# Chunked attention followed by a two-layer MLP: moving the attention output's transposes from TensorE to the DMA engines, and reordering the work around them

## The chip, the cores and the metric

The kernel runs on one core of one Trainium2 chip. The metric is device time in microseconds (us) for one execution. Before the change the median of 7 runs is 247.19 us (246.69 to 248.24). Profile times count from the start of the profiled span.

## The reference

Inputs `q`, `k`, `v` have 4 batches, 8 heads, 768 positions and 64 channels; each head has 8 memory keys and values besides. Each chunk of 32 queries attends to the memory slots and to the keys from 16 before the chunk to 8 after it. The attention output, seen as 3072 tokens of 512 channels, goes through an MLP with hidden width 2048:

```python
scores = scale * (q_c @ k_full.T)             # per batch, head, chunk of 32
a = softmax(scores); attn_out[chunk] = a @ v_full
x = attn_out.transpose(0, 2, 1, 3).reshape(3072, 512)
h = x @ w_in                                  # 512 -> 2048
g = h + sin(alpha * h) ** 2 / alpha
out = g @ w_out                               # 2048 -> 512, float32
```

## The kernel before

The kernel is one program whose order is written by hand; each engine executes its own instructions in the order in which the code records them. Matmul inputs are bf16.

**Stages.** For each of the four batches there are three kinds of work. A *burst* (`burst`) does the attention: 8 blocks of 96 queries. `qk_exp` makes the scores (8 matmuls, tile `sc`) and three exponentials on ScalarE (tile `pt`, line 275). `pv` multiplies by the values (8 matmuls, tile `ot`, line 288); VectorE then takes a reciprocal (L292) and scales into `x_blk` (L293), 96 queries by 512 channels. `xt` transposes `x_blk` on TensorE with four matmuls against an identity (L306) into PSUM, and VectorE copies them into `xT` (L309), which has channels on partitions. *Layer 1* (`l1`, 16 times per batch, once per 128 hidden columns `ft`): 8 matmuls (L341, tile `hT`), a sine on ScalarE (L353), a square into `s2` (letter A: ScalarE, L356; D: VectorE, L358; P: GpSimd), and one fused VectorE instruction (L367, or L363 in halves) that writes `gT`. *Layer 2* (`l2`): 6 groups of 16 matmuls (L393, tile `o`), each group then copied out of PSUM to `o_sb` (L400 VectorE or L402 ScalarE) and stored from SyncE's queue (L403).

**Interleaving.** Layer 2 of batch i is a generator in `stream`; `stream.take(n)` records n of its matmuls. They are spread over the layer 1 of the next batch (2 per `ft`), the burst of the next batch (`shares`, in thirds ahead of, between and behind the parts of a step), and, for batch 0, over the *pieces* of batch 1. A burst step s makes the scores of block s and the values of block s-lag; lag is 2, 3 and 1 for batches 0, 1 and later.

**Pieces.** `q` and `k` come in with positions on partitions. For each of 8 pieces per batch, `pair_up` copies a pair of heads to `pr` (L226), six TensorE transposes (L242 for k, L257 for q) go to a tile `tt_a` or `tt_b`, and VectorE copies k to `kTi` (L243, L249), ScalarE q to `qT` (L258). For batch 1 the pieces stand between layer 1 of batch 0 and burst 1; I call that stretch the *seam*. For batches 2 and 3 they stand between the `l1` calls of the batch before. For batch 0 they open the kernel, with `spin` matmuls on zeros between them.

**PSUM.** Pool `big` has 3 slots of two banks, in rotation, for `sc`, `ot`, `hT` and `tt_b`; pool `smp` has 2 slots of one bank for `o`, `tt_a`, `xtp`, the split `hs` and `spin`. `t_tile` takes `smp` every `state["pools"]`-th time. In the split form of `l1` (batch 0, every fourth `ft`) `hs` takes both `smp` slots.

**Loads.** `load_qk` and `load_v_all` for batch i+2 are issued from GpSimd's queue around burst i+1. They convert float32 to bf16.

Of the kernel before, what the change touches and what calls it, by code (L numbers as in the profile page):

```python
# [9 lines left out]
P = 128  # L10
QW = 96
NEG = -30000.0
KW = 856
BF = mybir.dt.bfloat16
F32 = mybir.dt.float32
ACTF = mybir.ActivationFunctionType
ALU = mybir.AluOpType
# [28 lines left out]
def kernel(  # L46
# [12 lines left out]
    nc = tc.nc  # L59
    B, H, S, D = q.shape  # L60
# [12 lines left out]
    xp = ctx.enter_context(tc.tile_pool(name="xp", bufs=2))  # L73
    gp = ctx.enter_context(tc.tile_pool(name="gp", bufs=2))
    mlp = ctx.enter_context(tc.tile_pool(name="mlp", bufs=3))
    blk = ctx.enter_context(tc.tile_pool(name="blk", bufs=3))
    big = ctx.enter_context(tc.tile_pool(name="big", bufs=3, space=bass.MemoryType.PSUM))
    smp = ctx.enter_context(tc.tile_pool(name="smp", bufs=2, space=bass.MemoryType.PSUM))

# [87 lines left out]
    def spin(n):  # L167

        z = smp.tile([P, 512], F32, name="z", tag="sm")
        for _ in range(n):  # L170
            nc.tensor.matmul(z[:], zeros[:, 0:P], zeros[:])  # L171
# [52 lines left out]
    def pair_up(src, hp, eng=None):  # L224
        pr = blk.tile([P, 6, 2, D], BF, name="pr")
        (eng or nc.gpsimd.tensor_copy)(  # L226
            pr[:].rearrange("p r e d -> p e r d"), src[:, 2 * hp:2 * hp + 2]
        )
        return pr
# [52 lines left out]
    def pv(b, j, pt):  # L282
        x_blk = blk.tile([QW, H, D], BF, name="x_blk")
        rinv = blk.tile([QW, H], F32, name="rinv")
        ot = big.tile([P, 2, 512], F32, name="ot", tag="big")
        otv = ot[:, :, 0:4 * (D + 1)].rearrange("p g (e c) -> p g e c", e=4)
        for h in range(H):
            nc.tensor.matmul(  # L288
                otv[:, h // 4, h % 4, :], pt[:, QW * h:QW * h + P], vws[b % 2][:, h, j, 0:D + 1]
            )  # L290
        rv = rinv[:].rearrange("p (g e) -> p g e", g=2)
        nc.vector.reciprocal(rv, otv[0:QW, :, :, D])  # L292
        nc.vector.tensor_tensor(  # L293
            out=x_blk[:].rearrange("p (g e) d -> p g e d", g=2), in0=otv[0:QW, :, :, 0:D],
            in1=rv.unsqueeze(3).to_broadcast([QW, 2, 4, D]),
            op=ALU.mult,
        )
        return x_blk, ot

    def xt(xT, j, x_blk, ot):  # L300
        if ot is None:
            xtp = smp.tile([P, KT, QW], BF, name="xtp", tag="sm")[:]
        else:
            xtp = ot[:].bitcast(BF)[:, 0, 640:640 + KT * QW].rearrange("p (k c) -> p k c", k=KT)
        for kt in range(KT):
            nc.tensor.transpose(  # L306
                xtp[:, kt, :], x_blk[:, 2 * kt:2 * kt + 2, :].rearrange("p e d -> p (e d)"), ident[0:QW, 0:QW]
            )
        nc.vector.tensor_copy(xT[:, :, QW * j:QW * j + QW], xtp)  # L309

    def burst(b, stream, shares, lag):

        xT = xp.tile([P, KT, S], BF, name="xT")
        ptl, xbl = {}, {}
        for s in range(NJ + lag + 1):
            n = shares[s] if s < len(shares) else 0
            if s < NJ:
                ptl[s] = qk_exp(s)
            if b == 0:
                spin(1)  # L320
            stream.take(n // 3, True)
            if 0 <= s - lag < NJ:
                xbl[s - lag] = pv(b, s - lag, ptl.pop(s - lag))
                if b == 0:
                    xbl[s - lag] = (xbl[s - lag][0], None)
            stream.take((n + 1) // 3, True)
            if 0 <= s - lag - 1 < NJ:
                xt(xT, s - lag - 1, *xbl.pop(s - lag - 1))
            stream.take((n + 2) // 3, True)
        return xT  # L330


    def l1(i, ft, xT, gT, sq, split=False):
        if split:
            hts = [smp.tile([P, 512], F32, name="hs", tag="sm") for _ in range(2)]
        else:
            hT = big.tile([P, 2, 512], F32, name="hT", tag="big")
            hts = [hT[:, 0], hT[:, 1]]
        for kt in range(KT):
            for hf in range(2):  # L340
                nc.tensor.matmul(  # L341
                    hts[hf][:, 0:HALF],
                    w_in_sb[:, kt, P * ft:P * ft + P],
                    xT[:, kt, HALF * hf:HALF * hf + HALF],
                    start=(kt == 0), stop=(kt == KT - 1),
                )
        u = mlp.tile([P, 2, HALF], F32, name="u")
        if split:
            for hf in range(2):
                nc.scalar.activation(  # L350
                    u[:, hf], hts[hf][:, 0:HALF], ACTF.Sin, scale=alpha_sb[:, ft:ft + 1])
        else:
            nc.scalar.activation(u[:], hT[:, :, 0:HALF], ACTF.Sin, scale=alpha_sb[:, ft:ft + 1])  # L353
        s2 = mlp.tile([P, 2, HALF], F32, name="s2")
        if sq == "A":
            nc.scalar.activation(s2[:], u[:], ACTF.Square)  # L356
        else:
            (nc.vector if sq == "D" else nc.gpsimd).tensor_tensor(  # L358
                out=s2[:], in0=u[:], in1=u[:], op=ALU.mult)
        gv = gT[:, ft, :].rearrange("p (e c) -> p e c", e=2)  # L360
        for hf in range(2):
            if split:
                nc.vector.scalar_tensor_tensor(  # L363
                    out=gv[:, hf], in0=s2[:, hf], scalar=inv_alpha[:, ft:ft + 1],
                    in1=hts[hf][:, 0:HALF], op0=ALU.mult, op1=ALU.add)
            elif hf == 0:
                nc.vector.scalar_tensor_tensor(  # L367
                    out=gv, in0=s2[:], scalar=inv_alpha[:, ft:ft + 1],
                    in1=hT[:, :, 0:HALF], op0=ALU.mult, op1=ALU.add)

    def l2(i, gT, last=False):
        for s in range(NSUB):
# [31 lines left out]
            yield True  # L404


    first = (nc.vector.tensor_copy, nc.scalar.copy)
    prs = [pair_up(kq[n], 0, first[n]) for n in range(2)]
    for n in range(2 * HP):
        (t_k if n % 2 == 0 else t_q)(prs[n], n // 2)  # L410
        spin(2)
        if n == 1:
            nc.scalar.copy(memv_st[64:72], memv_f[64:72])
            mt = smp.tile([P, HP, 32], BF, name="mt", tag="sm")
            for hp in range(HP):
                nc.tensor.transpose(
                    mt[:, hp, :],
                    memk_bf[0:32, 2 * hp:2 * hp + 2, :].rearrange("p e d -> p (e d)"),
                    ident[0:32, 0:32])
        if n + 2 < 2 * HP:  # L420
            prs.append(pair_up(kq[n % 2], (n + 2) // 2, first[n % 2]))
        if n == 1:
            nc.vector.tensor_copy(memkT[:], mt[:])
            put_memk(0)
        if n == 3:
            put_memv(0)
    put_memv(1)
    nc.vector.reciprocal(inv_alpha[:], alpha_sb[:])
    for c in range(8):
        load_w_in(c)  # L430
# [5 lines left out]
    stream = Stream()  # L436
    xT = burst(0, stream, (), 2)
    put_memk(1)

    for i in range(B):  # L440
        gT = gp.tile([P, FT, S], BF, name="gT")
        last = i == B - 1
        at_ft = {2 * n: n for n in range(8)}
        pieces = []
        if not last:
            srcs = [(kq_next[n % 2], n // 2) for n in range(2 * HP)]
        state["pools"] = 1

        def pair_to(n):
            while len(pieces) < min(n, 2 * HP):  # L450
                pieces.append(pair_up(*srcs[len(pieces)], nc.vector.tensor_copy if i == 0 else None))

        def piece(n):
            pair_to(n + 3)
            (t_k if n % 2 == 0 else t_q)(pieces[n], n // 2)

        if 0 < i < B - 1:
            pair_to(2)
        for ft in range(FT):
            sq = ("ADADADAA" if i == 0 else "ADADADAA")[ft % 8]  # L460
            if 1 <= ft:
                stream.take(3 if last else 2)
            if 0 < i < B - 1 and ft in at_ft:
                piece(at_ft[ft])
            if i == 0 and ft == 14:
                pair_to(3)
            l1(i, ft, xT, gT, sq, i == 0 and ft % 4 == 3)
        stream.add(l2(i, gT, last))
        if not last:
            if i == 0:  # L470
                state["pools"] = 3
                for n in range(2 * HP):
                    piece(n)
                    stream.take(4)
            if i + 2 < B:
                kq_next = load_qk(i + 2)
            if i == 0:
                xT = burst(i + 1, stream, (3,) * 11, 3)
            else:
                xT = burst(i + 1, stream, (12, 9, 6, 6, 6, 6, 6, 5, 5, 5), 1)  # L480
            if i + 2 < B:
                put_memk(i + 2)
            stream.take(3)
            if i + 2 < B:
                load_v_all(i + 2)
                put_memv(i + 2)
# [31 lines left out]
```

## Time and profile before

| what | value |
|---|---|
| median of 7 runs | 247.19 us (246.69 to 248.24) |
| the profiled execution's own time | 247.48 us |
| its span | 245.8 us |
| mean granted TensorE clock | 0.993 |
| L393 layer-2 matmuls, 368 | 99.9 us busy |
| L341 layer-1 matmuls (`hT`), 480 | 86.2 us busy |
| L306 transposes of `x_blk`, 128 | 10.8 us busy, of which 32 belong to batch 0 |
| L309 copies to `xT`, 32 | 11.1 us busy (346 ns each) |
| chain that ended last | PE 51%, DVE 20%, ACT 15%, issue 6%, POOL 5%, DMA 1% |

PE is TensorE, PEld its weight loads, DVE VectorE, ACT ScalarE, POOL GpSimd, SP SyncE. Busy time of PE counts pipelined matmuls with modelled ends that overlap, so what a matmul costs is better read from the distance between the starts of neighbours in a dense stretch. An arrow `<-` ahead of an instruction names what ended the engine's idle time before it.

### The profile page before, as it was taken

Reading aid. Unit: us, or ns where it says so; the run is one execution under the profiler, and the core shown is the slowest. Engines: PE = TensorE matmul, PEld = TensorE weight load, DVE = VectorE, ACT = ScalarE, POOL = GpSimd, SP = SyncE. Lnnn points to the kernel's source line nnn. Section 1 sums busy time; section 2 is a strip of 40 time slices with the busy share of each in tenths; the row PEclk is TensorE's granted clock in tenths of the full one; section 3 lists DMA queues with packets and bytes.
Section 4 is the critical chain, followed back from the end, with each engine's and each line's share of the span. In section 5 each row is a group of like instructions: output and inputs, shape, how many; then the busy total and the mean of one; then the engine's idle time right before and its main releaser. Section 6 shows DMA issues by size and latency. Waiting matters only on the chain.

```text
span 245.8 us, 4498 instructions
## 1 busy us (share of the span) xinstructions
PE 224.6 (91%) x1785; PEld 124.5 (51%) x1785; DVE 162.1 (66%) x290; ACT 161.0 (66%) x246; POOL 62.1 (25%) x86
## 2 busy tenths in 40 slices
PE   7787989984997999899899998999899999989994
PEld 2444645542644565555355555565355555544443
DVE  2466959998716879979465779888556277695101
ACT  0668949992378477887965477879865567974000
POOL 8899865100181231292100022100000000000000
PEclk9999999997999999999999999999999999999999
DMA  6999999999999940089951200101021101100122
GB/s 78 150 138 74 147 189 204 206 203 135 65 153 202 135 59 0 30 131 189 137 66 45 78 10 0 43 3 43 0 88 47 43 0 43 45 0 28 57 89 85
DMA packets 53853, 21.11 MB, mean 86 GB/s; under 512 B 36296, under 2 KB 50888, under 8 KB 53832
## 3 DMA queue, kind: packets, MB, share of 16 engines
q0 software_dynamic: 47616, 14.40, 70.7%
q1 hardware_dynamic: 6216, 6.43, 8.4%
q8 instruction: 14, 0.23, 0.4%
q14 instruction: 7, 0.06, 0.1%
HBM read 28.91 MB, written 6.29 MB: 143 GB/s over the span
## 4 chain that ended last, share of the span: by engine, by line
PE 51%; DVE 20%; ACT 15%; issue 6%; POOL 5%; DMA 1%; DVEq 0%; POOLq 0%; ACTq 0%
PE o L393 25%; PE hT L341 17%; DVE gT L367 6%; ACT pt L275 6%; DVE s L358 4%; ACT u L353 3%; DVE x_blk L293 3%; ACT s L356 3%; PE ot L288 2%; ACT L275 2%; PE o L382 1%; DVE kTi L243 1%; PE sc L266 1%; DVE xT L309 1%; PE tt_a L242 1%
## 5 line engine op out<-in xcount | busy, mean ns | idle before, releaser
L393 PE MATMUL o<-w_out_sb,gT 128*128 128x512 bf16 x368 | 99.9, 382 | 0.0
L341 PE MATMUL hT<-xT,w_in_sb 128*128 128x384 bf16 x480 | 86.2, 326 | 1.5 <-DVE gT L367 1.2
L367 DVE SCALAR_TENSOR_TENSOR gT<-s,inv_alpha,hT 128x768 bf16<-128x768 f32 x60 | 60.3, 1013 | 23.4 <-ACT s L356 21.1
L341 PEld LDWEIGHTS <-w_in_sb 128*128 128x128 bf16 x512 | 49.3, 98 | 36.3 <-issue 3.1
L353 ACT ACTIVATE u<-hT,alpha_sb 128x768 f32<-128x768 f32 x60 | 53.8, 898 | 21.1 <-PE hT L341 21.1
L393 PEld LDWEIGHTS <-gT 128*128 128x128 bf16 x368 | 32.1, 98 | 25.1 <-issue 0.5
L275 ACT ACTIVATE pt<-sc,biasm 128x256 bf16<-128x256 f32 x96 | 37.2, 493 | 11.0 <-PE sc L266 11.0
L356 ACT ACTIVATE s<-u 128x768 f32<-128x768 f32 x40 | 33.7, 844 | 1.3
L358 DVE TENSOR_TENSOR s<-u 128x768 f32<-128x768 f32 x24 | 26.3, 1095 | 0.6 <-ACT u L353 0.5
L292 DVE RECIPROCAL rinv<-ot 96x8 f32<-96x8 f32 x32 | 6.4, 201 | 25.0 <-PE ot L288 24.9
L293 DVE TENSOR_TENSOR x_blk<-ot,rinv 96x512 bf16<-96x512 f32 x32 | 22.0, 686 | 1.1
L402 ACT COPY o_sb<-o 128x512 f32<-128x512 f32 x11 | 6.4, 583 | 21.0 <-PE o L393 21.0
L226 POOL COPY pr<-q_bf 128x768 bf16<-128x768 bf16 x8 | 7.4, 923 | 49.7 <-PE tt_a L242 41.9
L288 PEld LDWEIGHTS <-pt 128*128 128x128 bf16 x256 | 11.7, 98 | 11.3 <-issue 4.2
L400 DVE COPY o_sb<-o 128x512 f32<-128x512 f32 x12 | 8.2, 685 | 13.8 <-PE o L393 13.8
L171 PE MATMUL z<-zeros 128*128 128x512 bf16 x37 | 15.8, 518 | 1.3 <-DVE zeros L165 1.3
L288 PE MATMUL ot<-vw,pt 128*128 128x65 bf16 x256 | 13.0, 193 | 3.5 <-ACT pt L275 2.5
L266 PEld LDWEIGHTS <-kTi 64*128 64x128 bf16 x256 | 7.0, 94 | 12.1 <-issue 6.1
L257 PEld LDWEIGHTS <-pr 128*128 128x128 bf16 x96 | 7.1, 108 | 10.8 <-ACT pr L226 5.0
L266 PE MATMUL sc<-qT,kTi 64*128 64x96 bf16 x256 | 11.2, 205 | 1.4 <-ACT pt L275 0.9
L242 PEld LDWEIGHTS <-pr 128*128 128x128 bf16 x96 | 7.4, 108 | 9.8 <-DVE pr L226 4.4
L306 PEld LDWEIGHTS <-x_blk 96*128 96x128 bf16 x128 | 8.2, 97 | 7.0 <-DVE x_blk L293 2.4
(65 smaller groups left out, 183.5 us busy)
## 6 DMA issues: line engine op xcount, KB each, us to landing
out_dram<-o_sb SPq DMA_DIRECT2D x23, 256.0 KB, 2.0
k_bf<-in_k_dram POOLq DMA_DIRECT2D x3, 768.0 KB, 7.4
q_bf<-in_q_dram POOLq DMA_DIRECT2D x3, 768.0 KB, 11.6
vw<-in_v_dram POOLq DMA_DIRECT2D x6, 384.0 KB, 17.0
w_in_sb<-in_moe_w_in_dram POOLq DMA_DIRECT2D x8, 256.0 KB, 8.3
w_out_sb<-in_moe_w_out_dram POOLq DMA_DIRECT2D x4, 512.0 KB, 18.5
k_bf<-in_k_dram POOLq DMA_DIRECT2D x4, 192.0 KB, 6.5
q_bf<-in_q_dram POOLq DMA_DIRECT2D x4, 192.0 KB, 6.7
```

What stands on the lines that cost most here:

```text
L171: nc.tensor.matmul(z[:], zeros[:, 0:P], zeros[:])
L242: nc.tensor.transpose(t[:, r, :], kb[:, r].rearrange("p e d -> p (e d)"), ident[:])
L266: nc.tensor.matmul(sc[:, e, QW * hp:QW * hp + QW], kTi[64 * e:64 * e + 64, hp, 104 * j:104 * j + P], qT[64 * e:64 * e + 64, hp, QW * j:QW ...
L275: nc.scalar.activation(pt[:, 0:H * QW].rearrange("p (g e c) -> p e g c", g=4, e=2)[:, :, :, 32 * m:32 * m + 32], sc[:, :, 0:4 * QW].rearra ...
L288: nc.tensor.matmul(otv[:, h // 4, h % 4, :], pt[:, QW * h:QW * h + P], vws[b % 2][:, h, j, 0:D + 1])
L293: nc.vector.tensor_tensor(out=x_blk[:].rearrange("p (g e) d -> p g e d", g=2), in0=otv[0:QW, :, :, 0:D], in1=rv.unsqueeze(3).to_broadcast( ...
L341: nc.tensor.matmul(hts[hf][:, 0:HALF], w_in_sb[:, kt, P * ft:P * ft + P], xT[:, kt, HALF * hf:HALF * hf + HALF], start=(kt == 0), stop=(kt ...
L353: nc.scalar.activation(u[:], hT[:, :, 0:HALF], ACTF.Sin, scale=alpha_sb[:, ft:ft + 1])
L356: nc.scalar.activation(s2[:], u[:], ACTF.Square)
L358: (nc.vector if sq == "D" else nc.gpsimd).tensor_tensor(out=s2[:], in0=u[:], in1=u[:], op=ALU.mult)
L367: nc.vector.scalar_tensor_tensor(out=gv, in0=s2[:], scalar=inv_alpha[:, ft:ft + 1], in1=hT[:, :, 0:HALF], op0=ALU.mult, op1=ALU.add)
L393: nc.tensor.matmul(o[:], gT[:, ft, P * s:P * s + P], w_out_sb[:, ft, :], start=(ft == 0), stop=(ft == FT - 1),)
```

## The change

The edits, in the order of the program:

1. Batch 0's pieces: the `pr` copies of the last two q pieces go to VectorE instead of ScalarE; the conversion of the memory values (`memv_st`, one ScalarE instruction) moves two pieces later, and the two copies of them into the value tiles move behind the pieces and behind burst 0.
2. Layer 1: VectorE's square and the fused instruction of an `ft` are recorded by `finish()`, which is called just before the matmuls of the next `ft`, so behind the `stream.take` and the piece between them. For `ft` 0 the eight matmuls run half by half: four on the first 384 positions, then four on the last 384. For batches 1 to 3 the 16 squares are 8 A, 6 D, 2 P instead of 10 A, 6 D. In batch 0 `ft` 15 is no longer split.
3. The seam: four layer-2 matmuls come first; then three (instead of four) behind each piece; the rotation of PSUM slots starts anew, so that the first two pieces take two-bank slots; q pieces' `pr` copies go to GpSimd. `blk` tiles get four buffers instead of three.
4. Bursts 1 to 3: no `L306` transposes and no `L309` copies. Each `x_blk` is transposed by a DMA from SyncE's queue straight into `xT`, issued in the step that makes `x_blk`. Batch 0 keeps the old way.
5. Shares of layer-2 matmuls: burst 1 takes 42 and then up to 8 more before the first `l1` (before: 33 and 3); bursts 2 and 3 take 57 and then 12 (before: 66 and 3).

```diff
-    blk = ctx.enter_context(tc.tile_pool(name="blk", bufs=3))
+    blk = ctx.enter_context(tc.tile_pool(name="blk", bufs=4))
...
     def xt(xT, j, x_blk, ot):
-        if ot is None:
-            xtp = smp.tile([P, KT, QW], BF, name="xtp", tag="sm")[:]
-        else:
-            xtp = ot[:].bitcast(BF)[:, 0, 640:640 + KT * QW].rearrange("p (k c) -> p k c", k=KT)
+        if ot is not None:
+            nc.sync.dma_start_transpose(
+                xT[:, :, QW * j:QW * j + QW], x_blk[:].rearrange("p h d -> p (h d)"))
+            return
+        xtp = smp.tile([P, KT, QW], BF, name="xtp", tag="sm")[:]
...
             if 0 <= s - lag < NJ:
-                xbl[s - lag] = pv(b, s - lag, ptl.pop(s - lag))
-                if b == 0:
-                    xbl[s - lag] = (xbl[s - lag][0], None)
+                x_blk, ot = pv(b, s - lag, ptl.pop(s - lag))
+                if b > 0:
+                    xt(xT, s - lag, x_blk, ot)
+                else:
+                    xbl[s - lag] = x_blk
...
+        order = [(kt, hf) for kt in range(KT) for hf in range(2)]
+        if ft == 0:
+            order.sort(key=lambda o: o[1])
...
-    first = (nc.vector.tensor_copy, nc.scalar.copy)
+    first = [nc.vector.tensor_copy, nc.scalar.copy] * 2 + [nc.vector.tensor_copy] * 4
...
-                pieces.append(pair_up(*srcs[len(pieces)], nc.vector.tensor_copy if i == 0 else None))
+                pieces.append(pair_up(*srcs[len(pieces)], nc.vector.tensor_copy if i == 0 and len(pieces) % 2 == 0 else None))
...
+        finish = None
         for ft in range(FT):
-            sq = ("ADADADAA" if i == 0 else "ADADADAA")[ft % 8]
+            sq = ("ADADADAAADADADAA" if i == 0 else "ADAAPDADADAPADAD")[ft]
...
-            l1(i, ft, xT, gT, sq, i == 0 and ft % 4 == 3)
+            if finish is not None:
+                finish()
+            finish = l1(i, ft, xT, gT, sq, i == 0 and ft in (3, 7, 11))
+        finish()
         stream.add(l2(i, gT, last))
         if not last:
             if i == 0:
-                state["pools"] = 3
+                state["pools"], state["t"] = 3, 0
+                stream.take(4)
                 for n in range(2 * HP):
                     piece(n)
-                    stream.take(4)
+                    stream.take(3, True)
...
             if i == 0:
-                xT = burst(i + 1, stream, (3,) * 11, 3)
+                xT = burst(i + 1, stream, (3, 3, 3, 4, 4, 4, 4, 4, 4, 4, 5), 3)
             else:
-                xT = burst(i + 1, stream, (12, 9, 6, 6, 6, 6, 6, 5, 5, 5), 1)
+                xT = burst(i + 1, stream, (16, 8, 5, 5, 5, 5, 5, 5, 3), 1)
...
-            stream.take(3)
+            stream.take(8 if i == 0 else 12)
```

More of the change, by code (lines that the diff above doesn't have):

```diff
@@ L322, in burst @@
             if 0 <= s - lag < NJ:
-                xbl[s - lag] = pv(b, s - lag, ptl.pop(s - lag))
-                if b == 0:
-                    xbl[s - lag] = (xbl[s - lag][0], None)
+                x_blk, ot = pv(b, s - lag, ptl.pop(s - lag))
[3 more added lines that the diff above has]
+                    xbl[s - lag] = x_blk
             stream.take((n + 1) // 3, True)
-            if 0 <= s - lag - 1 < NJ:
-                xt(xT, s - lag - 1, *xbl.pop(s - lag - 1))
+            if s - lag - 1 in xbl:
+                xt(xT, s - lag - 1, xbl.pop(s - lag - 1), None)
             stream.take((n + 2) // 3, True)
@@ L338, in l1 @@
             hts = [hT[:, 0], hT[:, 1]]
[L339 to L346, printed above, removed]
+        order = [(kt, hf) for kt in range(KT) for hf in range(2)]
+        if ft == 0:
+            order.sort(key=lambda o: o[1])
+        for kt, hf in order:
+            nc.tensor.matmul(
+                hts[hf][:, 0:HALF],
+                w_in_sb[:, kt, P * ft:P * ft + P],
+                xT[:, kt, HALF * hf:HALF * hf + HALF],
+                start=(kt == 0), stop=(kt == KT - 1),
+            )
         u = mlp.tile([P, 2, HALF], F32, name="u")
@@ L356, in l1, with finish @@
             nc.scalar.activation(s2[:], u[:], ACTF.Square)
[L357 to L369, printed above, removed]
+        elif sq == "P":
+            nc.gpsimd.tensor_tensor(out=s2[:], in0=u[:], in1=u[:], op=ALU.mult)
+        def finish():
+            if sq == "D":
+                nc.vector.tensor_tensor(out=s2[:], in0=u[:], in1=u[:], op=ALU.mult)
+            gv = gT[:, ft, :].rearrange("p (e c) -> p e c", e=2)
+            for hf in range(2):
+                if split:
+                    nc.vector.scalar_tensor_tensor(
+                        out=gv[:, hf], in0=s2[:, hf], scalar=inv_alpha[:, ft:ft + 1],
+                        in1=hts[hf][:, 0:HALF], op0=ALU.mult, op1=ALU.add)
+                elif hf == 0:
+                    nc.vector.scalar_tensor_tensor(
+                        out=gv, in0=s2[:], scalar=inv_alpha[:, ft:ft + 1],
+                        in1=hT[:, :, 0:HALF], op0=ALU.mult, op1=ALU.add)
+        return finish
     def l2(i, gT, last=False):
@@ L411 @@
         spin(2)
+        if n == 3:
+            nc.scalar.copy(memv_st[64:72], memv_f[64:72])
         if n == 1:
-            nc.scalar.copy(memv_st[64:72], memv_f[64:72])
             mt = smp.tile([P, HP, 32], BF, name="mt", tag="sm")
@@ L420 @@
         if n + 2 < 2 * HP:
-            prs.append(pair_up(kq[n % 2], (n + 2) // 2, first[n % 2]))
+            prs.append(pair_up(kq[n % 2], (n + 2) // 2, first[n + 2]))
         if n == 1:
@@ L424 @@
             put_memk(0)
-        if n == 3:
-            put_memv(0)
-    put_memv(1)
+    put_memv(0)
     nc.vector.reciprocal(inv_alpha[:], alpha_sb[:])
@@ L438 @@
     put_memk(1)
+    put_memv(1)
     for i in range(B):
```

## The prediction

> **What bounds the kernel now.** I read the page first, then busy times by stage, then the instructions in order of time inside one stage of each kind. From the page:
>
> ```profile
> PE 224.6 (91%) x1785; PEld 124.5 (51%) x1785; DVE 162.1 (66%) x290; ACT 161.0 (66%) x246; POOL 62.1 (25%) x86
> ...
> DMA  6999999999999940089951200101021101100122
> ```
>
> TensorE is the busiest engine, VectorE and ScalarE have a third of the span free on average. The DMA digits show the queues full in slices 2 to 14 (6 to 86 us) and again in slices 18 to 20 (104 to 123 us), nearly empty later. By stage (columns: stretch, its length, busy time and count of PE, PEld, DVE, ACT, POOL, then clock, DMA share, GB/s):
>
> ```profile
> 32.30:54.70 22.40, 21.71 (x132) 12.46 (x130) 18.66 (x25) 20.02 (x27) 7.54 (x9) 1.00 1.31 203
> 54.70:69.60 14.90, 11.03 (x81) 6.52 (x80) 11.06 (x26) 5.25 (x8) 2.62 (x3) 0.89 2.16 96
> 69.60:87.30 17.70, 15.54 (x202) 8.71 (x202) 10.00 (x27) 13.00 (x29) 5.82 (x7) 1.00 2.22 177
> 87.30:117.80 30.50, 29.82 (x203) 17.45 (x200) 26.53 (x34) 23.56 (x29) 13.36 (x14) 1.00 0.69 79
> 117.80:140.60 22.80, 21.81 (x235) 11.27 (x235) 13.33 (x30) 14.83 (x31) 0.09 (x1) 1.00 1.04 73
> 140.60:171.00 30.40, 29.36 (x202) 17.35 (x199) 26.10 (x34) 24.07 (x30) 4.22 (x5) 1.00 0.07 27
> 171.00:193.80 22.80, 21.81 (x232) 11.10 (x231) 12.55 (x28) 14.84 (x31) 0.00 (x0) 1.00 0.10 36
> 193.80:221.70 27.90, 27.04 (x157) 15.13 (x155) 19.66 (x21) 21.52 (x26) 0.00 (x0) 1.00 0.08 29
> 221.70:245.80 24.10, 20.89 (x113) 10.70 (x111) 4.99 (x7) 3.61 (x6) 0.00 (x0) 1.00 0.18 66
> ```
>
> These are layer 1 of batch 0, the seam, burst 1, layer 1 of batch 1, burst 2, layer 1 of batch 2, burst 3, layer 1 of batch 3, and the last layer 2. Only the seam and burst 1 leave TensorE visibly idle. One step of burst 2, TensorE's rows in order of time (start, busy us, what):
>
> ```profile
> 126.38 0.34 PE L266 MATMUL sc<-qT,kTi 64*128 64x96 bf16 x8
> ...
> 126.66 0.60 PE L393 MATMUL o<-w_out_sb,gT 128*128 128x512 bf16 x2
> ...
> 127.10 0.41 PE L288 MATMUL ot<-vw,pt 128*128 128x65 bf16 x8
> ...
> 127.34 0.59 PE L393 MATMUL o<-w_out_sb,gT 128*128 128x512 bf16 x2
> ...
> 127.77 0.34 PE L306 MATMUL ot<-ident,x_blk 96*128 96x96 bf16 x4
> ...
> 127.94 0.60 PE L393 MATMUL o<-w_out_sb,gT 128*128 128x512 bf16 x2
> ```
>
> Starts follow one another without a hole, so from their distances: scores of a block 0.28 us, values 0.24, the four transposes 0.17, two layer-2 matmuls 0.43. The chain of waits gives the dense price of the rest: 80 layer-2 matmuls in 17.32 us, 0.2165 each; 8 layer-1 matmuls 1.30 us; six transposes of a piece stand 0.33 us apart from what follows. Bursts 2 and 3 and layer 1 are bound by TensorE. The seam is not:
>
> ```profile
> 58.60 0.80 PE L242 MATMUL tt_a<-ident,pr 128*128 128x128 bf16 x6 [3.87 <-DVE gT L363]
> ```
>
> The first piece wants a one-bank slot, and both are held by the split `ft` 15 until VectorE has finished it: 3.87 us idle, after which the matmuls run slow for 2 us (0.43 us each).
>
> **What the Trainium skill says.** "DMA: Bandwidth & Descriptors", section "DMA Transpose (X-bar)" and the rules after it: a transposing DMA is issued from SyncE or ScalarE, and beside ordinary DMAs needs no ordering. No run here shows one yet. "VectorE: DVE Perf Modes", "The three transpose paths", gives 1309 ns for 128x128 bf16 by DMA against 390 on TensorE; pipelined, TensorE does four 96-wide ones in 0.17 us in this trace, so the gain is not in the transpose itself but in taking it off the full engine. "SBUF — State Buffer", "Who interferes with whom": a VectorE instruction with two SBUF inputs and a GpSimd one that reads SBUF exclude each other; the trace agrees, the square L358 takes 0.95 us at the median and up to 1.57 beside a GpSimd copy.
>
> **The change part by part**, against the profiled 245.8 us.
>
> *Opening.* ScalarE's serial chain (three `pr` copies of 0.83, the 1.90 conversion, `qT` copies of 0.80) sets when the first exponential starts (20.72). Two of the copies leave it and the conversion moves to where ScalarE waits. Followed through, the last `qT` copy ends near 19.5 instead of 20.36: -0.9. The moved VectorE copies (1.22 each) lie behind the last `kTi` copy and ahead of layer 1's first fused instruction (36.1): nothing, with idle VectorE as cover; 1.2 if not.
>
> *Seam.* Before, 14.9 us hold 32 layer-2 matmuls (6.9) and 8 pieces (2.6): 5.4 lost. After, 28 matmuls (6.1) and 2.6. The first four matmuls need only hidden tiles that are done. `ft` 15 now waits for a two-bank slot (about 0.9) and the first piece for the one of `ft` 13 (0.5); I leave 0.5 for the clock. So 10.6: -4.3. GpSimd's copies (0.92) replace VectorE's (0.36) with 1.9 us per pair to hide in. `w_out`'s last part is issued at 36.1 and lands 20.3 later, at 56.4; the thirteenth matmul needs it near 58: covered.
>
> *Burst 1.* After, 50 layer-2 matmuls (10.8) and 8 blocks at 0.28+0.24 (4.2): 15.0. The exponentials come 1.2 us apart from 3.2 us after the start, and a value tile waits for a two-bank slot; following the rotation I find 1.8 us of holes: 16.8. The transposes: from the last value matmul, 12 layer-2 matmuls (2.6) and the first half of `ft` 0 (0.65) pass before block 7 is needed, less reciprocal, scaling and semaphores (1.0): 2.25 us for the DMA. The nearest row is a store from the same queue:
>
> ```profile
> out_dram<-o_sb SPq DMA_DIRECT2D x4, 256.0 KB, 4.2
> ```
>
> That is the median in 66 to 90 us, while q, k and v of batch 2 fill the queues (extremes 2.0 and 6.3). A transpose moves 96 KB. I take 4.2: stall 2.0, so 18.8 for 17.7, +1.1. At 2.25 or less no stall (-0.9). At 6.3 the four `x_blk` buffers bind too: block 7 waits for block 3's, and lands 6.3 late (+5.4).
>
> *Layer 1 of batch 1.* Burst 1 took 14 more, the seam 4 fewer, so 18 instead of 28 remain: TensorE 20.8+2.6+3.9=27.3. VectorE: 16 fused at 1.01, 6 squares near 1.0, 4 `kTi` sets at 1.17, two copies at its start (1.4), one store copy: 28.9, part of it before the first sine. I take 28.5: -2.0.
>
> *Bursts 2 and 3.* Both kernels place 69 layer-2 matmuls here (14.9). Before 14.9+8x0.69=20.4 of 22.8; after 14.9+4.2=19.1. ScalarE ends layer 1 one square earlier and 16 matmuls stand ahead of the second scores, which closes the hole ahead of the first values (0.75). With 0.8 left of holes: 19.9, -2.9 each. Cover for the last transpose: 14 matmuls (3.0) plus 0.65 less 1.0 is 2.7; unloaded stores land in 2.0. Burst 2 has the loads beside its first half (a store there took 4.0), not at its end. VectorE loses 8 copies of 0.346.
>
> *Layer 1 of batches 2 and 3.* TensorE 20.8+2.6+5.8=29.3 of 30.4, and 26.7 of 27.9. With `finish` deferred, piece copies and store copies, whose inputs come first, no longer stand behind a wait for the sine: half the hole goes, -0.7 and -0.6. The six GpSimd squares have no row; low 0.83 (its bf16 copy), high 1.69, my estimate from "GPSIMD Engine Reference", 3.1 (4497 ns for 2048 elements, scaled to 768). With 1.69 the fused instruction ends 4.0 us after its matmuls, its slot is wanted after 4.4: hidden; uncovered up to 0.85 each, 5 in all. Below nothing: ScalarE is free of 0.84 each, but does not bind; no gain.
>
> SyncE's queue gets 24 transposes; stores stand behind them, each waiting for an `x_blk` at most a step away; four `o_sb` reuses lie further off than that: nothing. Sum: -0.9-4.3+1.1-2.0-2.9-2.9-0.7-0.6 = -13.2, span 232.6. The profiled execution's 247.48 becomes 234.3, and its median stands 0.29 lower: 234.0.
>
> **The rivals.** (B) *Transposes land late wherever loads run*: as worked out, 4.3 more in burst 1 and 1.4 more in burst 2 if it sees 4.0: 240, range 237 to 243. For it: full DMA digits over burst 1. Against: 96 KB is less than a store. (C) *They land inside the cover*: 2.0 better, and GpSimd's squares and the deferral take the other half of the holes: 230, 228.5 to 232. (D) *The transposes serialize, slower than before*: one block is four 96x128 pieces; at the skill's 1.31 us each, 5.2 us per block, 42 per burst against 20, +66 in three bursts: near 300. The point: from the first `x_blk` (5.5 us into burst 2) to the need of the last (20.2) there is room for 1.84 us per block at no cost, and for 2.4 until the 13.2 are gone. Against: the skill's figure is for one alone, and "Advanced Engine Details and Errata", "X-Bar Transpose (TRN2)", has them as fast as regular DMAs. (E) *Gains given back*: VectorE or PSUM slots bind layer 1 as soon as TensorE is relieved: 247. VectorE's 26.5 of 30.5 speaks for it in batch 1 only, and that is counted. That the transposes don't leave TensorE is excluded: the program has 24 fewer groups there and 24 transposes on SyncE's queue.
>
> **How the numbers follow.** Forecast (A) 0.50 (232 to 237), B 0.20, C 0.12, D 0.15, E 0.03. All of A, B and C are faster, with a tail each way in E: faster 0.83, same 0.02, slower 0.15 (0.3% is about what a measurement can tell). The range 229 to 243 holds A, B and most of C; D and E are left out.
>
> **What would show it.** Right: burst 2 near 20 us with steps of 1.6; no hole of over 1 us in the seam; burst 1 with a wait of TensorE on `xT` for a DMA of about 2 us; layer 1 of batch 1 near 28.5. Wrong: transposes over 2 us apart on SyncE's queue, waits of `x_blk` for a DMA, waits of `gT` for GpSimd over 1 us each.

## The result, and the profile after

The changed kernel takes 253.91 us (median of 12 runs, 251.64 to 255.75) against 247.15 (31 runs): 1.0258 times as long, 95% interval 1.0238 to 1.0278. The forecast was 234.0, the range 229 to 243. The sign was wrong. The profiled execution took 254.24 us, its span is 252.5. Medians here and below are of all executions, ratios leave out those over 1.5% above the fastest of the same kernel.

The page of the changed kernel, with the lines that answer to those of before (and the granted clock):

```profile
PE 221.9 (88%) x1689; PEld 120.6 (48%) x1689; DVE 152.7 (60%) x263; ACT 153.9 (61%) x237; POOL 73.7 (29%) x96
...
PEclk9999999999999769999999889999999799999999
DMA  6999999999999920016999700101143101100222
...
DMA packets 63836, 23.46 MB, mean 93 GB/s; under 512 B 46280, under 2 KB 60872, under 8 KB 63816
```

Every compute engine but GpSimd has less to do than before, and the kernel is slower: time went into waiting. Three dips of the clock (slices 14 and 15, 23 and 24, 32) were not there before. There are 63836 - 53853 = 9983 more DMA packets, 416 for each of the 24 transposes, nearly all under 512 B: a transpose is 98 KB in packets of some 235 B.

Busy time by stage, with the boundaries moved to where the stages now lie (seam, burst 1, layer 1 of batch 1, burst 2, layer 1 of batch 2, burst 3, layer 1 of batch 3; a burst is counted up to the second half of `ft` 0, which needs the last transpose):

```profile
54.70:62.60 7.90, 7.90 (x72) 4.92 (x71) 7.09 (x17) 3.64 (x5) 3.86 (x5) 1.00 3.70 130
62.60:89.60 27.00, 17.62 (x189) 8.67 (x189) 9.86 (x22) 12.99 (x29) 7.82 (x9) 0.92 1.82 158
89.60:118.80 29.20, 28.32 (x184) 16.68 (x184) 22.46 (x29) 22.60 (x28) 9.97 (x9) 0.95 0.14 29
118.80:144.00 25.20, 20.29 (x202) 9.81 (x202) 13.45 (x26) 14.47 (x30) 6.03 (x8) 0.99 1.68 155
144.00:175.80 31.80, 31.15 (x200) 18.01 (x201) 22.58 (x30) 22.61 (x28) 5.23 (x5) 0.95 0.06 24
175.80:197.60 21.80, 19.71 (x197) 9.54 (x197) 11.31 (x21) 14.65 (x30) 0.00 (x0) 1.00 0.29 77
197.60:228.40 30.80, 29.61 (x159) 15.93 (x160) 19.32 (x20) 20.18 (x24) 2.93 (x2) 0.94 0.07 25
```

| stage | before | forecast | after | transposes on TensorE, no GpSimd squares (e8) |
|---|---|---|---|---|
| start to burst 1 | 69.6 | 64.4 | 62.6 | 61.6 |
| burst 1 | 17.7 | 18.8 | 27.0 | 19.2 |
| layer 1, batch 1 | 30.5 | 28.5 | 29.2 | 29.2 |
| burst 2 | 22.8 | 19.9 | 25.2 | 21.1 |
| layer 1, batch 2 | 30.4 | 29.7 | 31.8 | 30.3 |
| burst 3 | 22.8 | 19.9 | 21.8 | 21.0 |
| layer 1, batch 3 | 27.9 | 27.3 | 30.8 | 29.0 |
| last layer 2 | 24.1 | 24.1 | 24.1 | 24.2 |

Only the column "after" counts the first half of `ft` 0, 0.65 us, to the burst; the others count it to layer 1. Bursts 1 and 2 miss by 13.5 us together (12.2 with that taken off); burst 3 and the layers 1 of batches 2 and 3 by 7.5. The view of waits (who waited, for what: us in total, times, longest) names the reason:

```profile
PE hT L346 <- DMA xT<-x_blk: 14.1, 5, 5.5
...
DVE x_blk L293 <- DMA xT<-x_blk: 13.8, 8, 2.8
```

TensorE stands still at the head of layer 1 until `xT` has landed, and VectorE stands still inside the bursts until an `x_blk` buffer has been read by its transpose. Landing in burst 1 (from issue; minimum, median, maximum of the blocks whose landing the profile tells, here three of eight; the instructions on `xT` between 66 and 90 us):

```profile
DMA to landing us min/median/max: 8.1/9.0/10.5
```

In burst 2 the median is 8.6 (of five blocks), in burst 3, where no loads run, it is 3.2 (of two). How the blocks follow one another in burst 2 is seen on VectorE, in order of time:

```profile
133.52 0.69 DVE L293 TENSOR_TENSOR x_blk<-ot,rinv 96x512 bf16<-96x512 f32 x1 [2.24 <-DMA xT<-x_blk]
...
136.00 0.69 DVE L293 TENSOR_TENSOR x_blk<-ot,rinv 96x512 bf16<-96x512 f32 x1 [1.68 <-DMA xT<-x_blk]
...
138.39 0.69 DVE L293 TENSOR_TENSOR x_blk<-ot,rinv 96x512 bf16<-96x512 f32 x1 [0.99 <-DMA xT<-x_blk]
...
140.89 0.69 DVE L293 TENSOR_TENSOR x_blk<-ot,rinv 96x512 bf16<-96x512 f32 x1 [1.69 <-DMA xT<-x_blk]
```

Each starts when a buffer comes free, and the starts are 2.4 to 2.5 us apart, where the burst makes a block every 1.7. SyncE's rows show where the 2.4 comes from:

```profile
124.81 5.74 SPq L302 DMA_TRANSPOSE xT<-x_blk  x3
130.64 0.53 SPq L413 DMA_DIRECT2D out_dram<-o_sb  x1
131.26 6.64 SPq L302 DMA_TRANSPOSE xT<-x_blk  x3
```

The first transpose of the burst is issued at 124.81, with no other transpose ahead of it, and its buffer comes free for the row at 133.52: 8.7 us. So the landing is long from the first block on; it does not grow out of a row of waiting transposes. With 0.75 us for scaling ahead of the issue (VectorE starts the burst's first `x_blk` at 124.06), a buffer is used once in 9.46 us, and four buffers make one block per 2.4 us. The last block meets the same long landing, and layer 1 waits for it.

The dips of the clock, asked for around each (stretch, length, PE busy, clock):

```profile
80.00:85.50 5.50, 1.30 (x11) 1.00 2.71 90
85.50:92.30 6.80, 2.68 (x8) 0.50 0.72 88
140.00:143.50 3.50, 0.82 (x4) 1.00 0.99 169
143.50:146.90 3.40, 2.87 (x8) 0.50 0.20 77
194.00:198.10 4.10, 2.04 (x13) 1.00 0.58 174
198.10:201.50 3.40, 3.40 (x10) 0.51 0.01 4
```

Each of these waits is followed by 3.4 or 6.8 us at half clock. In the last of them TensorE is busy throughout and gets half as much done, so 1.7 us are lost after the wait has ended; much of the first two falls into the wait itself. The prediction prices this in the seam only.

### The profile page after: what moved, and what is told of

It is laid out like the page before. It is cut to its first block, busy times and chain, and to the rows that moved or that the text cites. A ratio compares the mean times of both kernels' runs of the same rounds, so it can differ in the third digit from the quotient of the medians.

```text
span 252.5 us, 4349 instructions
## 1 busy us (share of the span) xinstructions
PE 221.9 (88%) x1689; PEld 120.6 (48%) x1689; DVE 152.7 (60%) x263; ACT 153.9 (61%) x237; POOL 73.7 (29%) x96
## 2 busy tenths in 40 slices
DMA packets 63836, 23.46 MB, mean 93 GB/s; under 512 B 46280, under 2 KB 60872, under 8 KB 63816
## 3 DMA queue, kind: packets, MB, share of 16 engines
q0 software_dynamic: 47616, 14.40, 64.4%
## 4 chain that ended last, share of the span: by engine, by line
PE 53%; DMA 14%; DVE 13%; ACT 8%; issue 8%; POOL 1%; POOLq 1%; SPq 0%; DVEq 0%; ACTq 0%
PE o L403 26%; PE hT L346 17%; DMA xT<-x_blk 12%; DVE gT L375 6%; ACT u L358 3%; PE sc L266 3%; DVE s L367 3%; DVE x_blk L293 2%; DMA q_bf<-in_q_dram 2%; ACT pt L275 2%; PE ot L288 2%; ACT s L361 2%; PE o L392 1%; POOL s L363 1%; PE tt_b L257 1%
## 5 line engine op out<-in xcount | busy, mean ns | idle before, releaser
L346 PE MATMUL hT<-xT,w_in_sb 128*128 128x384 bf16 x488 | 89.2, 330 | 18.0 <-DMA xT<-x_blk 14.1
L403 PE MATMUL o<-w_out_sb,gT 128*128 128x512 bf16 x368 | 97.6, 389 | 1.1 <-DVE o_sb L410 0.6
L358 ACT ACTIVATE u<-hT,alpha_sb 128x768 f32<-128x768 f32 x61 | 54.7, 898 | 45.2 <-PE hT L346 44.2
L403 PEld LDWEIGHTS <-gT 128*128 128x128 bf16 x368 | 34.0, 99 | 34.7 <-issue 4.4
L363 POOL TENSOR_TENSOR s<-u 128x768 f32<-128x768 f32 x6 | 8.8, 1465 | 102.9 <-ACT u L358 68.5
L361 ACT ACTIVATE s<-u 128x768 f32<-128x768 f32 x34 | 28.7, 843 | 1.1
L367 DVE TENSOR_TENSOR s<-u 128x768 f32<-128x768 f32 x24 | 24.4, 1016 | 5.2 <-ACT u L358 5.2
L226 POOL COPY pr<-q_bf 128x768 bf16<-128x768 bf16 x12 | 11.3, 947 | 16.3 <-PE tt_b L257 8.9
L226 POOL COPY pr<-k_bf 128x768 bf16<-128x768 bf16 x8 | 6.6, 823 | 19.2 <-PE tt_a L242 15.2
L242 PEld LDWEIGHTS <-pr 128*128 128x128 bf16 x96 | 6.9, 103 | 6.5 <-DVE pr L226 3.2
```

What stands on the lines that cost most here:

```text
L226: (eng or nc.gpsimd.tensor_copy)(pr[:].rearrange("p r e d -> p e r d"), src[:, 2 * hp:2 * hp + 2])
L346: nc.tensor.matmul(hts[hf][:, 0:HALF], w_in_sb[:, kt, P * ft:P * ft + P], xT[:, kt, HALF * hf:HALF * hf + HALF], start=(kt == 0), stop=(kt ...
L367: nc.vector.tensor_tensor(out=s2[:], in0=u[:], in1=u[:], op=ALU.mult)
L403: nc.tensor.matmul(o[:], gT[:, ft, P * s:P * s + P], w_out_sb[:, ft, :], start=(ft == 0), stop=(ft == FT - 1),)
```

## The experiments

My theory T after the trace: the DMA transposes cost the time, because they share the queues with the loads of q, k and v. The rival R: the reordering and the GpSimd squares cost it. Times are medians of 4 runs (20 for e3 and e5) beside runs of the kernel before on the same chip (246.9 to 247.3).

**e1: only the transposes back on TensorE.** `xt` and the burst loop are those of the kernel before, all else is the changed kernel.

```diff
-        if ot is not None:
-            nc.sync.dma_start_transpose(...)
-            return
+        else:
+            xtp = ot[:].bitcast(BF)[:, 0, 640:640 + KT * QW].rearrange("p (k c) -> p k c", k=KT)
```

> The changed kernel with only the transposes put back on TensorE (with the copy by VectorE, one step later, as before); shares, seam, deferred finish and GpSimd squares stay. Theory T (the DMA transposes cost the time: waits on xT and x_blk, and the half clock that follows each wait): burst 1 from 62.6 takes about 19.5 us, bursts 2 and 3 about 22 each, no wait on xT over 0.5 us, no half-clock stretch after a burst; span near 237, time near 238.5. Rival R (the reordering and the GpSimd squares cost it, TensorE's layer 1 stays at 31 to 32 us): 250 or more.

Measured: 237.16 us (236.81 to 237.82), 0.9595 of before (0.9561 to 0.9629). 16.8 us of the changed kernel's time hang on the transposes; the rest of the change is worth 10. R as the whole cause is out.

**e2: only the transposes moved, on the kernel before.** The reverse edit, with four `blk` buffers.

> The kernel before with only the transposes of batches 1 to 3 moved to DMA (and four buffers for blk tiles). T: there is less layer-2 work behind the last block than in the changed kernel, so the waits are longer: +9 in burst 1, +6 in burst 2, +3 in burst 3, near 264, at least 257. R: 245 to 250.

Measured: 254.58 us, 1.031 (1.026 to 1.0361). The sign is T's, the size is not: +7.6 where I expected +17. The waits on `xT` (11.2 us) and of `x_blk` (7.8) are smaller than in the changed kernel, and burst 2 meets hardly any loads: with no GpSimd square ahead of them, batch 3's are issued at 108.5, 17.6 us ahead of burst 2 (at 126.05), whose transposes then land in 2.3 us at the median. e3 tests that alone.

**e3: no GpSimd squares.**

```diff
-            sq = ("ADADADAAADADADAA" if i == 0 else "ADAAPDADADAPADAD")[ft]
+            sq = ("ADADADAAADADADAA" if i == 0 else "ADADADAAADADADAA")[ft]
```

> The changed kernel with no squares on GpSimd: batches 1 to 3 get the pattern of before (10 on ScalarE, 6 on VectorE). T: the six waits of VectorE for GpSimd sum to 6.5 us but lie beside TensorE's work; 252 to 254.5, within 1% of the changed kernel. R: 250 or less.

Measured: 247.97 us, 0.9996 (0.997 to 1.0021), 5.9 less than the changed kernel, against T, which had the squares as harmless. GpSimd's rows show how. The changed kernel:

```profile
113.33 1.47 POOL L363 TENSOR_TENSOR s<-u 128x768 f32<-128x768 f32 x1 [8.47 <-ACT u L358]
114.73 0.96 POOL L115 DMA_DIRECT2D k_bf<-in_k_dram  x1
```

And e3:

```profile
102.27 0.83 POOL L226 COPY pr<-q_bf 128x768 bf16<-128x768 bf16 x1 [2.97 <-PE tt_a L257]
103.04 0.90 POOL L115 DMA_DIRECT2D k_bf<-in_k_dram  x1
```

The square waits 8.47 us on GpSimd's queue for a sine, and batch 3's loads stand behind it: they are issued 11.7 us later, 4 us ahead of burst 2 instead of 17. In e3 burst 2's transposes land in 2.3 us at the median, and burst 2 takes 19.1 us to the head of layer 1.

**e4: no loads for batches 2 and 3.** Left out are the loads of q, k and v for these batches; they compute on the tiles of batches 0 and 1.

```diff
             if i + 2 < B:
-                kq_next = load_qk(i + 2)
+                pass
...
-                load_v_all(i + 2)
                 put_memv(i + 2)
```

> The changed kernel without the loads of q, k and v for batches 2 and 3; these batches compute on the tiles of batches 0 and 1 that are still there, so the output is another one and all instructions but the loads remain. T with load contention as the cause of the slow landing: transposes land in 2.3 to 4 us in all bursts, no x_blk waits for a DMA over 1 us, burst 1 and 2 lose their long waits: near 243. If the queue's own pace (1.2 us per transpose, in order behind stores) sets it: over 250.

Measured: 236.58 us, 0.9578 (0.9534 to 0.9622), the GpSimd squares still in. The waits shrink to:

```profile
PE hT L346 <- DMA xT<-x_blk: 3.7, 3, 1.7
...
DVE x_blk L293 <- DMA xT<-x_blk: 0.5, 1, 0.5
```

Transposes land in 2.3 us at the median, and no stretch at half clock follows a burst. Bursts 1 to 3 take 16.8, 19.1 and 18.9 us to the head of layer 1. So it is the loads beside the transposes, not the path from SyncE's queue as such: an issue takes 1.2 us of that queue with the loads and without. Nor is it the loads alone: e1 has the loads and no DMA transposes, and takes 237.2 us. 17.3 us less is more than I expected; the clock came back too, and how much of it that is was not measured.

**e5: only the later GpSimd square gone** (`"ADAAPDADADAAADAD"`).

> The changed kernel with the later of the two GpSimd squares of batches 1 to 3 (ft 11) on ScalarE. Theory L (the later square holds back the loads of batch 3, which stand behind it on GpSimd's queue, so that they run beside burst 2's transposes): the load of k is issued near 103 us as without any GpSimd square, burst 2 takes 19 to 20 us up to its second half, time near 248. Rival G (the GpSimd squares cost by themselves, through VectorE's waits): half of the difference, near 251, burst 2 still above 23.

Measured: 247.29 us, 1.0003 (0.9978 to 1.0028), as e3. The three GpSimd squares that are left still keep VectorE waiting (4.5 us in all) and cost nothing; k is issued at 105.3. What cost was the load behind the square; e8 bears this out.

**e6: 8 dummy matmuls between the halves of `ft` 0**, so that TensorE is less idle.

```diff
         for kt, hf in order:
+            if ft == 0 and i > 0 and (kt, hf) == (0, 1):
+                spin(8)
             nc.tensor.matmul(
```

> The changed kernel with 8 dummy matmuls on zeros between the two halves of ft 0 in batches 1 to 3, where TensorE waits for the last transposes. Theory C (idle of TensorE of more than about 2 us is followed by a stretch at half clock, which is a cost of its own): the 1.7 us of dummies lie inside the waits; the half-clock stretches behind bursts 2 and 3 are gone or moved, 1.7 us each: near 250.5. If the clock is lowered for another reason: 253 to 256.

Measured: 252.57 us, four runs from 248.44 to 254.04 (1.0108, 1.0018 to 1.0197); too wide to tell 250.5 from 253.9. The same stretches behind bursts 2 and 3 in its trace (the profiled execution took 253.7):

```profile
143.80:147.30 3.50, 2.85 (x14) 1.32 (x15) 3.13 (x6) 0.00 (x0) 0.00 (x0) 1.00 0.52 153
196.30:201.00 4.70, 4.70 (x25) 2.24 (x24) 0.00 (x0) 3.28 (x4) 0.00 (x0) 1.00 0.33 93
```

Full clock, where the changed kernel had half. That dummies keep the clock up is likely from this, not shown: in other traces it stayed up without them (e7). What it is worth in the whole time was not settled.

**e7: loads held back until a burst's last transpose has landed**, no GpSimd squares, pieces at `ft` 7 to 14.

```diff
+                gate = mlp.tile([P, QW], BF, name="gate")
+                nc.gpsimd.tensor_copy(gate[:], xT[:, 0, S - QW:S])
+                kq_next = load_qk(i + 2)
                 put_memk(i + 2)
...
-        at_ft = {2 * n: n for n in range(8)}
+        at_ft = {n + 7: n for n in range(8)}
```

> The changed kernel with no GpSimd squares, and with the loads of q, k and v for batch i+2 held back until the last transpose of burst i+1 has landed (a small GpSimd copy of that block ahead of them); the pieces stand at ft 7 to 14 instead of 0, 2 to 14. T: bursts as without the loads (16.8, 19.1 and 18.9 us), nothing waits for a transpose over 2 us, layer 1 takes 29 to 31: near 238. If the transposes are slow for another reason than the loads beside them: over 245.

Measured: 240.31 us, 0.9729 (0.9677 to 0.9781). The loads are all there, only later, and the transposes land in 2.3 us at the median. 2 us short of what I expected: TensorE still waits up to 2.4 us for `xT` after a burst. The loads' new place is not the only edit here: against e3, which also has no GpSimd squares, e7 is 7.7 us faster, with the pieces moved as well. Around the longest of these waits, which ends at 184.34 (stretch, length, PE busy, clock):

```profile
181.50:185.00 3.50, 1.13 (x8) 1.00 0.53 148
184.34:188.00 3.66, 3.66 (x20) 1.00 0.15 57
```

No dip: a wait as long as the 2.06 us behind burst 3 of the changed kernel need not cost the clock. This trace is of the shortest of the four executions (238.67 us, granted clock 0.993); the two of 241 us had 0.979, so the clock may have fallen in them.

**e8: e1 without GpSimd squares.**

> The transposes on TensorE, all else as in the changed kernel, but no GpSimd squares. With the transposes off the DMA queues, late loads have nothing to disturb: L gives the same as with the GpSimd squares, 236.5 to 238. G (they cost by themselves): 233 or less.

Measured: 237.18 us, 0.9587 (0.9551 to 0.9624), as e1. k is issued at 93.3 us here and at 105.1 in e1, and it makes no difference, since no transpose is on the DMA queues.

**e9: e8 with DMA transposes in batch 3 only**, and 16 layer-2 matmuls behind its last block.

> The fastest so far (transposes on TensorE, no GpSimd squares) with the DMA transposes in batch 3 only, where no loads run, and 16 layer-2 matmuls behind the last block. T: burst 3 takes 18.9 us plus 3.5 for the 16 matmuls instead of 7, less 1.5, no wait on xT over 1 us, no half clock: 235.5 to 236.5, a little under the 237.2 with all on TensorE. If the DMA path costs even without loads: 238 or more.

Measured: 237.74 us (237.52 to 237.85), 0.9621 (0.9597 to 0.9646): a miss. No wait on `xT` in burst 3 and full clock throughout in the trace, and still no gain: the median of the four spans is 235.45 us, that of e8's 235.35. The executions take 1.8 to 3.0 us beyond their spans, e8's 1.8. Why is open.

**e10: e8 without the deferral** (`finish` called at once).

> The same base (transposes on TensorE, no GpSimd squares) with VectorE's square and fused instruction recorded right behind each layer 1 again, as in the kernel before. My step gave the deferral about 0.6 us per batch in batches 1 to 3: near 239. If the deferral does nothing: 237.2. If it holds the two-bank slots longer and costs: 235 to 236.

Measured: 240.28 us, 0.9746 (0.9693 to 0.9798): 3.1 us more than e8 for the lack of the deferral, more than I gave it. Layer 1 of batch 1 takes 31.4 us instead of 29.2, that of batch 2 31.5 instead of 30.3.

**e11: eight buffers for `x_blk`** in the changed kernel.

> The changed kernel with eight buffers for x_blk instead of four. Theory Q (the transposes are one queue with a pace of 2.4 us under load, so the last lands when it does): waits of x_blk for a DMA vanish, waits of the layer-1 matmuls on xT grow by as much; within 1% of the changed kernel, 252 to 255. Rival S (the wait for a free x_blk buffer is itself the loss): 248 or less.

Measured: 252.75 us, 1.0209 (1.0156 to 1.0262). No wait of `x_blk` for a DMA is left, but TensorE's and its weight loads' waits on `xT`, 17.1 us together, are only 1.5 longer than in the changed kernel:

```profile
PE hT L347 <- DMA xT<-x_blk: 14.7, 5, 5.4
PEld L347 <- DMA xT<-x_blk: 2.4, 1, 2.4
```

The time falls within theory Q's range, but Q's pace of 2.4 us is not there. Burst 1 of e11, its transposes (first and last start), their landing, and the end of TensorE's wait:

```profile
L303 SPq DMA_TRANSPOSE xT<-x_blk x8: 1208/1277/2144, 67.2 to 79.9; - x8
...
DMA to landing us min/median/max: 9.2/9.3/9.6
...
88.22 1.44 PE L347 MATMUL hT<-xT,w_in_sb 128*128 128x384 bf16 x4 [5.41 <-DMA xT<-x_blk]
```

Eight blocks are issued 1.8 us apart, as fast as the burst makes them, and the last, 8.3 us after its issue, is no later behind it than the others. So 2.4 us was four buffers divided into a long landing, as in the result above. But the burst is no shorter (26.8 us, from 61.46, for 27.0): buffers are not the loss, rival S is out, and the long landing under load is. In e11 the last block is issued 2.8 us earlier in the burst than in the changed kernel, and lands no earlier. Whether each block's own landing sets that, or all that loads and transposes move together, is not told apart.

**e12: the opening and the seam alone**, on the kernel before.

> The kernel before with the changed opening and seam alone (piece copies, memory-value copies, ft 15 not split, PSUM slots anew, 4 plus 3 per piece). My step: 0.9 and 4.3 less, 0.9 of layer-2 work handed on to later: near 242. The stages of the changed kernel say more, burst 1 starts 7 to 8 us earlier: near 240. If the gain is given back later: 246.

Measured: 242.72 us, 0.9838 (0.98 to 0.9875). Layer 1 of batch 0 starts at 28.8 instead of 32.4 and burst 1 at 61.2 instead of 69.6; 4.0 of these 8.4 us are given back later. The four layer-2 matmuls that the seam no longer holds account for 0.9 of it, as expected; the rest shows as longer layers 1 of batches 1 and 2 (32.8 and 31.9 us for 30.4 each), for a reason that stays open.

**e13: the cover behind bursts 2 and 3 in full.** `stream.take(12)` ends at the end of a group of 16; after the 57 of the burst that is 7.

```diff
-            stream.take(8 if i == 0 else 12)
+            stream.take(8 if i == 0 else 12, i > 0)
```

> The changed kernel with the 12 layer-2 matmuls behind bursts 2 and 3 recorded in full: as written, the call stops at the end of a group of 16 and records 7, and the other 5 follow behind ft 0. Theory K (the missing 1.1 us of cover makes burst 3's wait of 2.1 us, and that wait the half-clock stretch behind it): burst 3's wait falls to about 1 us, its half-clock stretch (1.7 us lost) goes, burst 2 keeps its own because its wait is longer: 251.5 to 252.5. If the cover doesn't matter: 253 to 255.

Measured: 252.31 us (249.81 to 253.43), 1.0235 (1.0164 to 1.0306). Burst 3's wait falls from 2.1 to 0.4 us, and behind it:

```profile
194.00:198.50 4.50, 4.08 (x24) 2.08 (x22) 0.00 (x0) 3.37 (x4) 0.00 (x0) 1.00 0.27 81
198.50:202.00 3.50, 3.50 (x21) 1.95 (x20) 2.99 (x3) 2.25 (x4) 0.00 (x0) 1.00 0.00 0
```

Full clock, 21 matmuls in 3.5 us, where the changed kernel did 10 in 3.4. The dip behind burst 2 stays, as its wait does. The times of e13 and of the changed kernel overlap, so what this is worth in all is not measured.

**e14: e7 with 10 and 16 layer-2 matmuls behind the last block, in full.**

> The kernel with DMA transposes and the loads held back until a burst's last transpose has landed, now with 10 (burst 1) and 16 (bursts 2 and 3) layer-2 matmuls behind the last block, recorded in full, instead of 8 and 7. T: no wait on xT over 0.5 us where 2.4 was the longest; 238 to 239.5, from 240.3. Then what is left against TensorE's transposes (237.2) is the bunching of the pieces in ft 7 to 14. If the waits were hidden already: 240.3, if the moved layer-2 work is missed in layer 1: over 240.5.

Measured: 235.72 us (234.90 to 236.15), 0.9544 (0.9491 to 0.9596). One wait on `xT` is left, in burst 1:

```profile
PE hT L346 <- DMA xT<-x_blk: 1.8, 1, 1.8
```

This is the fastest version found; its four runs lie below all of e1's and e8's, though the intervals of the ratios overlap. So with the loads off the queues and the last landing covered, the DMA transposes are no longer a loss. That they gain is not shown: the difference to e8 is 1.5 us, e14 also has more cover and the pieces at other places, which were not tried with TensorE's transposes, and e9, with DMA transposes, no loads and cover in batch 3, gains nothing.

## Why the prediction was wrong

The step that failed is *Burst 1*: "The nearest row is a store from the same queue", and from it "I take 4.2: stall 2.0". Measured, a block took 8.1 to 10.5 us to land there, and the stretch 27.0 us (26.4 in the forecast's count) instead of 18.8. The mechanism of the step is the one that acted: a landing longer than its cover leaves TensorE waiting, and "the four `x_blk` buffers bind too". Its size was wrong, beyond the 6.3 us that I allowed, and so was the reason for it: "96 KB is less than a store" says nothing of the landing, for a block of 98 KB took longer than any of the stores of 256 KB that I had read (2.0 to 6.3 us). The same term failed in burst 2, where the median was 8.6.

That is rival B, "Transposes land late wherever loads run", with a longer landing than B was priced at; its range ended at 243. Rival D, "The transposes serialize", is not what the traces show: the first block of a burst landed as late as the others, and in e11 blocks went through 1.8 us apart beside the loads. D's price of 5.2 us per block was my estimate from the 1309 ns for 128x128 in the Trainium skill, "VectorE: DVE Perf Modes", "The three transpose paths". No run has such a single transpose; a whole 96x512 block landed 2.3 us after its issue without loads, so four of them end to end are not its price. What its "Advanced Engine Details and Errata", "X-Bar Transpose (TRN2)", says, as fast as regular DMAs, comes near for a block alone (2.3 us in e4, against 2.0 for an unloaded store) and was no guide beside loads. What the packets of loads and transposes do to each other inside the DMA engines is not shown; that the loads are the cause is (e4, and e7 against e3).

*GpSimd's squares*: "hidden; uncovered up to 0.85 each". Their duration (1.47 us, between my bounds) and VectorE's waits are hidden, as said (e5). What I left out is the queue behind them: "Burst 2 has the loads beside its first half, not at its end" holds only if they are issued where they were before. The square moved them 11.7 us, into most of burst 2: some 6 to 7 us (e3, e5).

*Cover behind bursts 2 and 3*: "14 matmuls (3.0)". There are 9: the call returns at the end of a group. With the cover in full, burst 3's wait falls from 2.1 to 0.4 us (e13). The five matmuls, 1.1 us, stand in the layers 1 of batches 2 and 3, which take 30.3 and 29.0 us in e8 for 29.7 and 27.3; what else lengthens the last is open. Read in the order of the built program, not in the argument of the call, it would have been seen.

*The clock*: not priced outside the seam. Behind burst 3 it costs 1.7 us (10 matmuls in 3.4 us, 21 in 3.5 at full clock in e13); behind bursts 1 and 2 part of it.

*Opening and seam*: right in mechanism. The seam came as forecast: 9.2 us from its first matmul, and 1.1 of wait ahead of `ft` 15, for 10.6. The opening gave more: the first exponential starts at 18.51, 2.2 us earlier, for 0.9. Burst 1 starts 7.0 us earlier, for 5.2. In e12 both together are worth 4.4 us. *Layer 1 of batch 1*: 28.5 forecast, 29.2 measured, with 2.7 us of it at half clock and the first half of `ft` 0 counted before it. *Deferral*: right, 3.1 us for some 2 (e10). *Bursts with the transposes off TensorE*: 19.1 and 18.9 us in e4 for 19.9. Rival E is not what happened: relieved of the transposes' waits, the rest kept its gain (e1). Of the forecast's own marks of being wrong, "waits of `x_blk` for a DMA" came true as written, and "transposes over 2 us apart" where the buffers held them back. The "waits of `gT` for GpSimd over 1 us each" came true on average (6.5 us in six waits), but these waits cost nothing by themselves (e5, e8).

## What to carry to other kernels

Before moving work to a DMA, look at what else is on the DMA queues at that time, and take the landing from a transfer of the same kind under that load, or take it as unknown: the landing of the last transfer must fit into its cover. A long landing also ties up the buffers (here 9.46 us over four of them, for a step of 1.7), but more buffers alone did not help (e11). An instruction that waits on an engine's queue holds back the loads issued behind it, and those land where they hurt (e3). With the loads moved away and the cover counted in the built program, the same idea stops losing (e14).

## What was not expected of the hardware

At half clock TensorE stayed for 3.4 us or twice that, and no length of the wait alone decides it. Behind waits of 2.06 us (changed kernel) and 2.10 (e3), both at burst 3, the clock fell; behind 2.26 (e11) and 2.37 (e7), at the same place, it did not, nor behind 1.74 and less (e4). The waits of 2.8 and 5.5 us in burst 1 of the changed kernel both have it. The Trainium skill, "TensorE: Matmul & The Clock Gate", Part 1, says that the clock is set by activity in a window of about 3.4 us that runs free of the kernel. The stretches of 3.4 and 6.8 us agree with that, and so does the scatter between equal waits; that the phase of the window decides was not tried. The page names an idle window as what lowers the clock; here a full one wasn't needed, as the waits near 2 us show.

A transposed block of 98 KB took 2.3 us at the median from issue to landing with no load beside it (e4), and 8.1 to 10.5 us beside loads (burst 1 of the changed kernel), late from the first block on (8.7 us in burst 2). The issue itself took 1.2 us of SyncE's queue in both.
